# Two unused stretches of memory and eight overwritten products in an attention and mixture kernel

## The chip, the core and the metric

The kernel runs on one core of a Trainium2 chip. The core has a matrix engine (PE, with its weight loads shown apart as PEld), a vector engine (DVE), a scalar engine (ACT), GpSimd (POOL), a queue engine that issues the transfers (SP), an on-chip memory of 128 partitions, and a memory for the sums of the products (PSUM). The metric is the device time of one execution in microseconds; three runs of the kernel before gave 735.54, 736.54 and 736.76 us, a median of 736.54.

## The reference

Attention over 8 batches, 12 heads, 448 positions and 64 columns a head, with scores squeezed by a tanh, and behind it a gated mixture of 768 to 1024 to 512 to 768 columns:

```python
scores = scale * np.matmul(q, k.transpose(0, 1, 3, 2))
scores = cap * np.tanh(scores / cap)
attn = np.exp(scores - max); attn = attn / (sum + 1e-09)
x = (attn @ v) as (batch, 448, 768)
h = np.maximum(x @ w_in, 0.0)
u, v = h[..., :512], h[..., 512:]
v_n = (v - mean(v)) / sqrt(var(v) + 1e-06)
v_s = w_spatial applied over positions to v_n, + b_spatial
out = (u * v_s) @ w_out
```

## The kernel before

A condition on the cap picks one of two forms of the program; the inputs here take the "bounded" one. Each batch has three groups of four heads (`quad_bnd`) and one mixture (`moe`).

In a group the scores are products of 64x64 weights by 448 columns in float32 (L592), ACT takes their tanh (L596) and exponential (L603), and PE multiplies by v (L613). DVE folds the exponentials into maxima and sums (L631, L639, L641); the result goes through memory and comes back as a factor, by which DVE multiplies the group's output (L696). `halves` then splits each pair of heads into a high part (ACT, L353) and a low part (DVE, L349) in a tile `xg`; both parts are numbers of a 32-bit form that PE multiplies in one pass (float32r).

A mixture has four kinds of products, all of full 128x128 weights, three products for each pair of split operands:

- u part (L749 to L751): weights `wi1_h`, `wi1_l`, moving operand `xg`, 448 columns; 4 blocks of 18 products a batch, so 72.
- v part (L771 to L776): weights `xg`, moving operand `wi2_h`, `wi2_l`, 512 columns; 66 a batch.
- spatial part (L840 to L845): weights `vh`, `vl`, moving operand `ws_h`, `ws_l`, 448 columns; 44 a batch.
- output part (L865 to L867): weights `wo_h`, `wo_l`, moving operand `xg`, 448 columns; 72 a batch.

The weights of w_in, w_spatial and w_out are split into their high and low parts in the first batch, by POOL, DVE and ACT, beside the attention (`split_f64`, `split_f32`).

The order of all this is settled when the program is built: `Plan.order` simulates the engines with the costs given to `add`, and takes on each engine the ready task with the lowest key. Each engine then runs its list in that order. A task's function may issue several instructions, which stay together; the task's cost is a number in the call, not counted from them. The first mixture starts with its u part (`V_FIRST` is 1, and the first batch is 0), and its first chain is block j = 0, whose task c = 0 issues three products, then c = 1, and so on; they share the sum tile `acc`.

The tiles of a pool lie one behind the other in each partition, in the order in which they are allocated. Taken modulo 256 bytes, their addresses are these (worked out from the tiles' sizes; every tile that is not named in the change keeps its size):

| tiles | before | with the change |
|---|---|---|
| raw, wi2, ws, red, sh, st | 0 | 0 |
| wi1, wo, dt, one | 0 | 192 |
| v, tp, xf, rr, xg, u, stg | 128 | 0 |
| vh, vl, o | 64 | 192 |

Offsets inside a tile that these products use are multiples of 256 bytes. The distance, modulo 256 bytes and in the shorter direction, between the weights of a product and the operand that streams is therefore: u part 128, then 64; v part 128, then 0; spatial part 64, then 64; output part 128, then 64. In the attention's products (raw with raw, v with tp) it stays as it was.

Of the kernel before, what the change touches and what calls it, by code (L numbers as in the profile page):

```python
# [9 lines left out]
F32 = mybir.dt.float32  # L10
# [6 lines left out]
B, H, S, D = 8, 12, 448, 64  # L17
# [25 lines left out]
class Plan:  # L43
# [15 lines left out]
    def add(self, eng, dur, key, fn, deps=(), uses=(), allocs=(), lat=0.0, name="", mode="N"):  # L59
        t = Task()  # L60
        t.eng, t.dur, t.key, t.fn, t.lat, t.name, t.mode = eng, float(dur), key, fn, lat, name, mode
        t.lock = eng == "P" or eng == "V" and name not in self.OWN
        t.deps = [d for d in deps if d is not None]
        t.allocs = list(allocs)
        t.uses = list(dict.fromkeys(list(uses) + t.allocs))
        for u in t.uses:
            u.users += 1
        t.seq = len(self.tasks)
        self.tasks.append(t)
        return t  # L70
# [123 lines left out]
def act(n, extra=0):  # L194

    return 0.833 * n + 51 + 93 * extra
# [63 lines left out]
               wi5=1.1376, wi6=13.0344, wi7=2.468, wi8=-18.9783, wi9=3.3202, wi10=-13.2504, wi11=-12.154, ws0=-12.654,  # L260
               ws1=-7.9959, ws2=-33.2129, ws3=-10.2049, wo0=-6.4452, wo1=-0.8201, wo2=2.6051, wo3=8.6589)
BND_V_FIRST = 1
WARM, WARM_N = 14, 512
BND_W_KEYS = -14.6272, 0.1578, -3.1507, 14.803, -4.1788, 0.5729, 0.2535
SPARE = ()
PE_SUMS = 3
# [7 lines left out]
def attn_moe(ctx, tc, bounded, shared, qk, v, qk2, v2, cap, w_in, w_sp, w_out, out):  # L274
    nc = tc.nc
# [4 lines left out]
    def pool(name, bufs, space=None):  # L280
        kw = {"space": space} if space else {}
        return ctx.enter_context(tc.tile_pool(name=name, bufs=bufs, **kw))

    const = pool("const", 1)
# [27 lines left out]
    def weights(name, parts, width):  # L312
        return [const.tile([128, parts, width], F32R, name=f"{name}_{p}") for p in "hl"]
# [3 lines left out]
    if bounded:  # L317

        def keep(tag, n, width, fill=None):
            own[tag] = [const.tile([128, width], F32, name=f"{tag}{i}") for i in range(n)]  # L320
            for t in own[tag]:
                if fill is not None:
                    nc.gpsimd.memset(t, fill)

        keep("red", RED, 2 * PW)
        keep("sh", DEN, 64, 1.0)
        keep("st", DEN, 64, 1.0)
    wi1_h, wi1_l = weights("wi1", NP, FH)
    wo_h, wo_l = weights("wo", 4, DM)
    if bounded:  # L330
        keep("dt", DEN, 64, 1.0)
        one = const.tile([128, D + 32], F32, name="one")[:, :D]
        nc.gpsimd.memset(one, 1.0)

    if not bounded:
# [386 lines left out]
    def chain(k, units, acc):  # L722

        prev = None
        for i, (dur, fn, deps, uses) in enumerate(units):
            prev = add("T", dur, k, fn, [prev, *deps], [*uses, acc], [acc] if i == 0 else [], name="moe")
        return prev

    def moe(b, xs):
# [10 lines left out]
        def u_part(js):  # L740
            for j in js:
                k = next(ks)
                acc, u = Buf(next(tags)), Buf("u")
                fs = slice(j * 128, (j + 1) * 128)

                def um(c, acc=acc, fs=fs):
                    x = xs[c][0].t
                    ps = acc.t[:, 0, :S]
                    nc.tensor.matmul(ps, lhsT=wi1_h[:, c, fs], rhs=x[:, XH:], start=(c == 0), stop=False)  # L749
                    nc.tensor.matmul(ps, lhsT=wi1_h[:, c, fs], rhs=x[:, :S], start=False, stop=False)  # L750
                    nc.tensor.matmul(ps, lhsT=wi1_l[:, c, fs], rhs=x[:, XH:], start=False, stop=(c == NP - 1))  # L751

                l = chain(k, [(3 * MM, lambda c=c, um=um: um(c), wi_t[c] + xdep[c], xuse[c:c + 1]) for c in range(NP)], acc)
                r = add("A", act(448), kv(k), lambda acc=acc, u=u: nc.scalar.activation(out=u.t, in_=acc.t[:, 0, :S], func=AF.Relu),
                        [l], [acc], [u], name="urelu")
                us.append((u, r))
# [66 lines left out]
        if b >= V_FIRST:  # L823
            v_part()
            u_part(range(U_LEAD))
        else:
            u_part(range(U_LEAD))
            v_part()
        for j in range(4):
            if j and j + U_LEAD <= 4:  # L830
                u_part([j + U_LEAD - 1])
            k = next(ks)
            acc, gt, g = Buf(next(tags)), Buf("o"), Buf("xg")
            fs = slice(j * 128, (j + 1) * 128)

            def gm(c, acc=acc, fs=fs):
                vh, vl = vs[c][:2]
                ps = acc.t[:, 0, :S]
                if c == 3:
                    nc.tensor.matmul(ps, lhsT=vh.t[:97, fs], rhs=ws_l[:97, c, :], start=False, stop=False)  # L840
                    nc.tensor.matmul(ps, lhsT=vl.t[:, fs], rhs=ws_h[:, c, :], start=False, stop=True)
                    return
                nc.tensor.matmul(ps, lhsT=vh.t[:, fs], rhs=ws_h[:, c, :], start=(c == 0), stop=False)  # L843
                nc.tensor.matmul(ps, lhsT=vh.t[:, fs], rhs=ws_l[:, c, :], start=False, stop=False)  # L844
                nc.tensor.matmul(ps, lhsT=vl.t[:, fs], rhs=ws_h[:, c, :], start=False, stop=False)  # L845

            l = chain(k, [((2 if c == 3 else 3) * MM, lambda c=c, gm=gm: gm(c), ws_t[c] + [vs[c][2]], vs[c][:2])
                          for c in range(4)], acc)
            u, ur = us[j]
            m = add("V", dve(448), kv(k), lambda acc=acc, gt=gt, u=u: nc.vector.tensor_mul(gt.t, acc.t[:, 0, :S], u.t), [l, ur],  # L850
                    [acc, u], [gt], name="gmul")

            e0, e1 = E_G
            c_ = add(e0, ct(e0, 448), kv(k), lambda gt=gt, g=g: copy(e0, g.t[:, XH:], gt.t), [m], [gt], [g], name="gcopy")
            d = add(e1, st2(e1, 448), kv(k), lambda gt=gt, g=g: sub(e1, g.t[:, :S], gt.t, f(g.t[:, XH:])), [c_], [gt, g], name="gl")
            gs.append((g, d))
        for q in range(6):
            k = next(ks)
            acc, o = Buf(next(tags)), Buf("o")
# [30 lines left out]
def either(ctx: ExitStack, tc: tile.TileContext, *args):  # L890
# [24 lines left out]
    with tc.If(bits <= CAP_BITS) as cmp:  # L915
        with ExitStack() as es:
            attn_moe(es, tc, True, shared, *args)
    with cmp.Else():
        with ExitStack() as es:
            attn_moe(es, tc, False, shared, *args)  # L920
# [29 lines left out]
```

## Time and profile before

| | |
|---|---|
| median of 3 runs | 736.54 us (735.54 to 736.76) |
| the profiled execution | 735.65 us |
| its span, first to last instruction | 733.8 us |
| mean granted clock of PE | 0.992 |
| PE busy | 718.4 us (98%) |
| DVE busy | 601.6 us (82%) |
| ACT busy | 480.0 us (65%) |
| POOL busy | 80.9 us (11%) |

The profiled execution is 0.89 us below the median of the runs. A granted clock of 1.00 is 2.4 GHz and 0.50 is 1.2 GHz. Products overlap, so one product's own duration (0.36 us for 448 columns) is longer than the distance from its start to the start of the next (about 0.20 us); what a product costs in a dense stretch is read from that distance.

### The profile page before, as it was taken

How to read it: one execution, taken by the hardware profiler on the slowest of the kernel's cores; microseconds unless marked ns; L12 is line 12 of the kernel's file. 1: busy time of each engine (PE TensorE's matmuls, PEld its weight loads, DVE VectorE, ACT ScalarE, POOL GpSimd, SP SyncE). 2: the span in 40 equal slices, each digit the busy share in tenths (PEclk: the TensorE clock that was granted, in tenths of full speed). 3: DMA queues.
4: the chain of work that ended last, by engine and by line, in shares of the span. 5: the costliest groups of instructions: out<-in, count | busy, mean ns of one | idle time of the engine just before them, and what ended most of it. 6: DMA issues, size and time to landing. Idle time of an engine off the chain costs nothing.

```text
span 733.8 us, 12258 instructions
## 1 busy us (share of the span) xinstructions
PE 718.4 (98%) x4902; PEld 488.2 (67%) x4902; DVE 601.6 (82%) x849; ACT 480.0 (65%) x648; POOL 80.9 (11%) x71
## 2 busy tenths in 40 slices
PE   8996999999999999999999999999999999999997
PEld 3332676575668656786558688568565865698896
DVE  4899999999999989948999996299799688982520
ACT  6999657849784884649875833785876678324321
POOL 2234411600110001000120001000020000200100
PEclk9998999999999999999999999999999999999999
DMA  8565314424221441033330420213321131102002
GB/s 278 163 207 157 111 35 139 161 93 143 69 77 50 132 122 50 26 102 101 101 87 22 155 92 26 63 63 129 101 76 41 60 116 38 52 17 86 1 1 80
DMA packets 34263, 66.50 MB, mean 91 GB/s; under 512 B 6034, under 2 KB 21908, under 8 KB 34196
## 3 DMA queue, kind: packets, MB, share of 16 engines
q1 hardware_dynamic: 34196, 65.62, 28.1%
q8 instruction: 40, 0.66, 0.4%
q14 instruction: 27, 0.22, 0.1%
HBM read 54.40 MB, written 11.18 MB: 89 GB/s over the span
## 4 chain that ended last, share of the span: by engine, by line
PE 88%; DVE 5%; ACT 2%; DMA 2%; issue 1%; SPq 1%; POOL 0%; DVEq 0%; ACTq 0%
PE ps_s L592 15%; PE ps_x L613 15%; PE ps_acc L749 5%; PE ps_acc L750 5%; PE ps_acc L751 5%; PE ps_acc L865 5%; PE ps_acc L866 5%; PE ps_acc L867 5%; PE ps_acc L774 4%; PE ps_acc L776 4%; PE ps_acc L775 4%; PE ps_acc L843 2%; PE ps_acc L844 2%; PE ps_acc L845 2%; DVE red L631 2%; PE ps_acc L771 2%
## 5 line engine op out<-in xcount | busy, mean ns | idle before, releaser
L596 ACT ACTIVATE tp<-ps_s,capt 128x896 f32<-128x896 f32 x168 | 162.5, 1005 | 29.7 <-PE ps_s L592 22.2
L631 DVE TENSOR_TENSOR red<-red,tp 128x1792 f32<-128x1792 f32 x90 | 140.9, 1566 | 23.4 <-ACT tp L603 21.7
L603 ACT ACTIVATE tp<-tp,capt 128x1792 f32<-128x1792 f32 (+1 forms) x96 | 154.1, 1607 | 1.5
L592 PE MATMUL ps_s<-raw 64*64 64x448 f32 x1344 | 146.9, 545 | 3.5 <-ACT tp L596 3.3
L613 PE MATMUL ps_x<-tp,v 64*64 64x448 f32 x1344 | 140.0, 536 | 0.5 <-ACT tp L603 0.4
L631 DVE TENSOR_TENSOR red<-tp 128x1792 f32<-128x1792 f32 x45 | 91.2, 2027 | 13.8 <-ACT tp L603 12.9
L613 PEld LDWEIGHTS ps_x<-tp,v 64*64 64x64 f32 x1344 | 51.2, 133 | 75.9 <-issue 68.7
L592 PEld LDWEIGHTS ps_s<-raw 64*64 64x64 f32 x1344 | 47.4, 133 | 79.3 <-issue 47.5
L798 POOL TENSOR_TENSOR lst<-lst,capt 128x1 f32<-128x1 f32 x32 | 35.0, 1095 | 532.1 <-DVE lst L796 532.0
L749 PE MATMUL ps_acc<-xg,wi_h 128*128 128x448 f32 x180 | 67.5, 375 | 3.1 <-ACT xg L353 3.1
L750 PE MATMUL ps_acc<-xg,wi_h 128*128 128x448 f32 x180 | 66.8, 371 | 0.4 <-DVE xg L349 0.4
L751 PE MATMUL ps_acc<-xg,wi_l 128*128 128x448 f32 x180 | 66.4, 369 | 0.0
L865 PE MATMUL ps_acc<-xg,wo_h 128*128 128x448 f32 x176 | 65.1, 370 | 0.0
L866 PE MATMUL ps_acc<-xg,wo_h 128*128 128x448 f32 x176 | 64.5, 367 | 0.6 <-DVE xg L349 0.6
L867 PE MATMUL ps_acc<-xg,wo_l 128*128 128x448 f32 x176 | 64.4, 366 | 0.0
L353 ACT CAST xg<-o 128x448 fp32r<-128x448 f32 x32 | 18.1, 567 | 53.3 <-DVE o L850 47.8
L774 PE MATMUL ps_acc<-wi_h,xg 128*128 128x512 f32 x126 | 50.6, 402 | 0.0
L639 DVE STREAM_TRANSPOSE red<-red 128x896 f32<-128x896 f32 x45 | 49.6, 1102 | 0.7
L776 PE MATMUL ps_acc<-wi_h,xg 128*128 128x512 f32 x126 | 49.7, 395 | 0.0
L775 PE MATMUL ps_acc<-wi_l,xg 128*128 128x512 f32 x126 | 49.7, 394 | 0.0
L641 DVE TENSOR_REDUCE st<-red 128x28 f32<-128x896 f32 x45 | 48.6, 1079 | 0.7
L631 DVE TENSOR_TENSOR red<-red 128x896 f32<-128x896 f32 x45 | 48.6, 1081 | 0.6
(144 smaller groups left out, 1112.3 us busy)
## 6 DMA issues: line engine op xcount, KB each, us to landing
raw<-in_qk SPq DMA_DIRECT2D x48, 448.0 KB
rr<-rd SPq DMA_DIRECT2D x48, 224.0 KB
out<-o SPq DMA_DIRECT2D x48, 224.0 KB
w<-in_w_in SPq DMA_DIRECT2D x12, 512.0 KB
v<-in_v SPq DMA_DIRECT2D x24, 256.0 KB
v<-in_v SPq DMA_DIRECT2D x24, 192.0 KB
xg<-in_w_out SPq DMA_DIRECT2D x12, 256.0 KB
rd<-dt SPq DMA_DIRECT2D x48, 3.5 KB
```

What stands on the lines that cost most here:

```text
L592: nc.tensor.matmul(ps.t[c * D:(c + 1) * D, e, :S], lhsT=f(raw[c].t)[r, k:k + D], rhs=f(raw[c].t)[r, :S], start=True, stop=True)
L596: th = add("A", act(PW, 1), kk("th", i), lambda ps=ps, tp=tp, o=o: nc.scalar.activation(out=tp.t[:, o:o + PW].rearrange("p (e q) -> p e q" ...
L603: ex = add("A", act_s(w, 1), kk("ex", i), lambda tp=tp, w=w: nc.scalar.activation(out=tp.t[:, :w], in_=tp.t[:, :w], func=AF.Exp, scale=ca) ...
L613: nc.tensor.matmul(x.t[e * D:(e + 1) * D, c, :S], lhsT=vts[g // 2].t[c * D:(c + 1) * D, (4 * (g % 2) + 2 * j + e) * D:(4 * (g % 2) + 2 * j ...
L631: nc.vector.tensor_tensor(o_(), i0(), i1(), op=op)
L749: nc.tensor.matmul(ps, lhsT=wi1_h[:, c, fs], rhs=x[:, XH:], start=(c == 0), stop=False)
L750: nc.tensor.matmul(ps, lhsT=wi1_h[:, c, fs], rhs=x[:, :S], start=False, stop=False)
L751: nc.tensor.matmul(ps, lhsT=wi1_l[:, c, fs], rhs=x[:, XH:], start=False, stop=(c == NP - 1))
L774: nc.tensor.matmul(ps, lhsT=x[:, XH:][:, ts], rhs=wi2_h[:, c], start=(c == 0), stop=False)
L865: nc.tensor.matmul(ps, lhsT=wo_h[:, c, ns], rhs=g[:, XH:], start=(c == 0), stop=False)
L866: nc.tensor.matmul(ps, lhsT=wo_h[:, c, ns], rhs=g[:, :S], start=False, stop=False)
L867: nc.tensor.matmul(ps, lhsT=wo_l[:, c, ns], rhs=g[:, XH:], start=False, stop=(c == 3))
```

## The change

Two things change. A tile `gap` of 192 bytes that nothing reads or writes is allocated between the tiles `st` and `wi1`, and the tile `one`, of which 256 bytes are used, is made 192 bytes longer at its end. So `wi1`, `wo`, `dt` and `one` move by 192 bytes, and all tiles behind `one` by 384 (the table above).

The first task of the first mixture's first chain issues eight more products ahead of its own three: weights `wi1_h` by 448 columns of `wi1_h`, into the chain's sum tile, each started afresh. The chain's own first product starts afresh too and overwrites them. The task's cost in the plan stays as it was, and so does the order of all other instructions.

```diff
-WARM, WARM_N = 14, 512
+WARM, WARM_N, FILL = 14, 512, 8
...
+    if bounded:
+        const.tile([128, 48], F32, name="gap")
     wi1_h, wi1_l = weights("wi1", NP, FH)
     wo_h, wo_l = weights("wo", 4, DM)
...
-        one = const.tile([128, D + 32], F32, name="one")[:, :D]
+        one = const.tile([128, D + 80], F32, name="one")[:, :D]
...
+                fill = FILL if bounded and b == 0 and j == 0 else 0
...
-                def um(c, acc=acc, fs=fs):
+                def um(c, acc=acc, fs=fs, fill=fill):
                     x = xs[c][0].t
                     ps = acc.t[:, 0, :S]
+                    for _ in range(fill if c == 0 else 0):
+                        nc.tensor.matmul(ps, lhsT=wi1_h[:, 0, fs], rhs=wi1_h[:, 0, :S], start=True, stop=True)
                     nc.tensor.matmul(ps, lhsT=wi1_h[:, c, fs], rhs=x[:, XH:], start=(c == 0), stop=False)
```

On PE, at the start of the first mixture, there stood before (raw is the operand of the scores, ps_s their sums):

```order
L592 MATMUL ps_s<-raw_60 64x448 x2
L592 MATMUL ps_s<-raw_61 64x448 x2
L592 MATMUL ps_s<-raw_60 64x448 x2
L592 MATMUL ps_s<-raw_61 64x448 x2
L749 MATMUL ps_acc<-xg,wi_h 128x448
L750 MATMUL ps_acc<-xg,wi_h 128x448
L751 MATMUL ps_acc<-xg,wi_l 128x448
L749 MATMUL ps_acc<-xg,wi_h 128x448
```

Now there stands on PE at the same place (line numbers behind the first edit are 2 to 5 higher):

```order
L594 MATMUL ps_s<-raw_60 64x448 x2
L594 MATMUL ps_s<-raw_61 64x448 x2
L594 MATMUL ps_s<-raw_60 64x448 x2
L594 MATMUL ps_s<-raw_61 64x448 x2
L753 MATMUL ps_acc<-wi_h 128x448 x8
L754 MATMUL ps_acc<-xg,wi_h 128x448
L755 MATMUL ps_acc<-xg,wi_h 128x448
L756 MATMUL ps_acc<-xg,wi_l 128x448
L754 MATMUL ps_acc<-xg,wi_h 128x448
```

The eight products stand between the last scores and the chain's first product. They wait for no other engine: the wait for `xg` stays on the product behind them. On all engines, no other instruction changes its place.

## Rows read from the trace of the kernel before

**Rows 1.** The page: engines' busy time, and the chain that ended last by engine.
```profile
PE 718.4 (98%) x4902; PEld 488.2 (67%) x4902; DVE 601.6 (82%) x849; ACT 480.0 (65%) x648; POOL 80.9 (11%) x71
PE 88%; DVE 5%; ACT 2%; DMA 2%; issue 1%; SPq 1%; POOL 0%; DVEq 0%; ACTq 0%
```

**Rows 2.** Waits of PE, whole span: total us, times, longest us.
```profile
PE ps_s L592 <- ACT tp L596: 3.3, 2, 2.9
PE ps_acc L749 <- ACT xg L353: 3.1, 1, 3.1
...
PE ps_acc L750 <- DVE xg L349: 0.4, 1, 0.4
```

**Rows 3.** Stretches: length, busy us of each engine, granted clock (first after POOL), DMA.
```profile
67.00:69.00 2.00, 1.81 (x12) 0.30 (x8) 2.00 (x6) 2.00 (x2) 0.00 (x0) 0.50 0.03 4
69.00:71.90 2.90, 0.00 (x0) 0.00 (x0) 2.32 (x5) 2.90 (x9) 0.00 (x0) 0.50 0.76 214
74.00:76.90 2.90, 2.90 (x9) 2.60 (x8) 2.90 (x5) 2.87 (x4) 1.50 (x2) 0.50 0.50 200
77.10:152.40 75.30, 74.56 (x536) 47.89 (x534) 74.08 (x128) 50.23 (x72) 22.73 (x17) 1.00 0.33 101
152.40:727.00 574.60, 574.58 (x3760) 412.21 (x3761) 464.68 (x629) 360.39 (x494) 32.37 (x28) 1.00 0.24 74
```

**Rows 4.** PE in order of time, around the first chain: start, duration, idle before.
```profile
66.14 2.67 PE L592 MATMUL ps_s<-raw 64*64 64x448 f32 x16 [2.89 <-ACT tp L596]
71.95 0.74 PE L749 MATMUL ps_acc<-xg,wi_h 128*128 128x448 f32 x1 [3.14 <-ACT xg L353]
73.06 0.74 PE L750 MATMUL ps_acc<-xg,wi_h 128*128 128x448 f32 x1 [0.36 <-DVE xg L349]
73.60 0.57 PE L751 MATMUL ps_acc<-xg,wi_l 128*128 128x448 f32 x1
73.97 0.57 PE L749 MATMUL ps_acc<-xg,wi_h 128*128 128x448 f32 x1
...
76.96 0.41 PE L751 MATMUL ps_acc<-xg,wi_l 128*128 128x448 f32 x1
77.20 0.36 PE L749 MATMUL ps_acc<-xg,wi_h 128*128 128x448 f32 x1
```

**Rows 5.** Waits of DVE from 62 to 153 us, all of them.
```profile
DVE wy L422 <- POOL wy L418: 0.6, 1, 0.6
DVE xg L349 <- ACT xg L353: 0.6, 1, 0.6
DVE vh L809 <- issue: 0.2, 1, 0.2
```

**Rows 6.** Waits of PE from 140 to 153 us; there are none later.
```profile
PE ps_acc L866 <- DVE xg L349: 0.6, 1, 0.6
PE ps_x L613 <- ACT xf L619: 0.2, 1, 0.2
```

**Rows 7.** PE in the last mixture: first and last product of four unbroken stretches.
```profile
674.89 0.39 PE L774 MATMUL ps_s<-wi_h,xg 128*128 128x512 f32 x1
...
690.00 0.40 PE L772 MATMUL ps_acc<-wi_l,xg 128*128 128x512 f32 x1
690.23 0.37 PE L749 MATMUL ps_acc<-xg,wi_h 128*128 128x448 f32 x1
...
697.37 0.37 PE L751 MATMUL ps_s<-xg,wi_l 128*128 128x448 f32 x1
...
709.34 0.37 PE L843 MATMUL ps_s<-ws_h,vh 128*128 128x448 f32 x1
...
713.60 0.37 PE L841 MATMUL ps_s<-ws_h,vl 128*128 128x448 f32 x1
713.80 0.36 PE L865 MATMUL ps_x<-xg,wo_h 128*128 128x448 f32 x1
...
728.28 0.36 PE L867 MATMUL ps_x<-xg,wo_l 128*128 128x448 f32 x1
```

## The prediction

> **What bounds the kernel now.** I read the page's busy times and its chain first: PE is busy 98% of the span and makes up 88% of the chain that ended last [rows 1]. So the question is where PE is not the bound, and at what speed it runs where it is. The list of PE's waits answers the first: two long waits for ACT, of 2.9 and 3.1 us [rows 2], both in the neighbourhood of the first mixture, and then only small ones, the last of them 0.6 us for DVE at about 152 us [rows 6]. The view by stretches puts a border there. From 152.4 to 727 us PE is busy 574.58 of 574.60 us, DVE only 464.68 and ACT 360.39: PE alone is the bound. From 77.1 to 152.4 us both PE (74.56) and DVE (74.08 of 75.30 us) are full [rows 3], and DVE's own waits there name POOL (0.6 us) and issue (0.2 us), never PE or an ACT step that follows PE; its other wait, 0.6 us for ACT, lies before 77 us [rows 5]. So up to 152 us DVE runs at its own pace, splitting weights and folding the attention, and PE stands at the border waiting for a DVE result. What PE saves before the border meets DVE there; what it saves behind it reaches the end.
>
> The clock is the third thing to see. It is 0.50 (1.2 GHz) from 67 us on, after the 2.89 us wait, through the second wait and the first half of the chain, and 1.00 again at 77.1 us [rows 3, 4].
>
> **The eight products.** PE's last scores ahead of the chain run from 66.14 for 2.67 us, so to 68.81. The chain's first product starts at 71.95, after 3.14 us of waiting for ACT [rows 4]. The eight products fall into that hole, since they wait for nobody. At the low clock a product of 448 columns starts every 0.37 us (73.60 to 73.97 in rows 4), so eight take 8 x 0.373 = 2.98 us and end at 71.8 us, 0.15 us ahead of the time at which `xg` is there; if the clock rises on the way they end earlier. Cover: the wait for ACT, which does not depend on PE. If that cover were 0.1 to 0.2 us shorter, the chain would start that much later.
>
> What they give: PE is then busy from 66.14 us nearly without a break. Before, the clock came back at about 77.0 us, after PE had worked without a break since 73.06. With the break filled it should be back by about 71 to 74 us. The second product still waits for DVE until 73.06. From 73.60 to 76.96 there are nine distances of 0.373 us, and one of 0.24 to 77.20 [rows 4]; at the 0.204 us of the full clock (below) the nine save 9 x 0.169 = 1.52 us, and with the distances on either side some 1.8 us. So at 80 us PE should be 1.8 us ahead.
>
> What is late next: DVE. In 77.1 to 152.4 us it has 75.30 - 74.08 = 1.22 us without work. Its listed waits take 0.8 of that, none of them for PE; the rest, 0.4 us, is the most that could shrink if PE's results came sooner. So PE gives the 1.8 us back in waits for DVE (and for ACT behind DVE) before the border. The bounds on what reaches the end are 0.2 us lost (the cover gone, and nothing passed on) and 0.4 us won. I take 0.1 us won, near the low end, since the rows name no wait for PE.
>
> **The two stretches.** They add no instruction. What they can change is the speed of the products whose two operands now lie otherwise to each other. The trace has a natural comparison: before the change the spatial part is 64 bytes apart already, the three others 128. Distances from start to start, in the last mixture, at the full clock [rows 7]: u part, 36 products, (697.37 - 690.23) / 35 = 204.0 ns; output part, 72 products, (728.28 - 713.80) / 71 = 203.9 ns; spatial part, 22 products, (713.60 - 709.34) / 21 = 202.9 ns. All have 448 columns. The v part, 66 products of 512 columns: (690.00 - 674.89) / 65 = 232.5 ns. So a product 64 bytes apart is 1.1 ns faster than one 128 apart, with about 0.5 ns of doubt, since the rows go by 10 ns.
>
> After the change the u and output parts are 64 apart. In the seven mixtures behind the border that is 7 x (72 + 72) = 1008 products, so 1008 x 1.1 = 1.1 us, all on PE where nothing else is the bound. The spatial part stays 64 apart: nothing. The v part goes from 128 to 0 apart, 7 x 66 = 462 products, which no stretch of the trace shows. Its cost is bounded by how much such a product stalls at all: 448 columns at 2.4 GHz are 186.7 ns, so some 17 ns of 204 are lost, and for 512 columns 19 ns of 232.5. At the low clock nothing is lost (0.373 us is 448 columns at 1.2 GHz). If all of it went, the v part would give 462 x 19 = 8.8 us; if it doubled, it would cost as much. As 64 and 128 bytes differ by 1.1 ns only, I take nothing for 0. For the u and output parts the same ends are -1008 x 17 = -17.1 us and +17.1; I take the value of the spatial part, the nearest row. DVE, ACT and the transfers: their tiles move together or by 128 bytes against `red`; for them the bounds are small against the 110 us that DVE has idle behind the border, so I cost them at nothing.
>
> The Trainium skill ("TensorE: Matmul & The Clock Gate", section "Step-by-step: what each phase is for") speaks against any effect: streaming and weight loading have independent read ports, and loading weights takes nothing from a running product. By that rule the second term would be nothing and the sum -0.1 us. The measured 1.1 ns between the parts speaks weakly against the rule, so it stands below as a rival.
>
> **The sum.** -0.1 (eight products) - 1.1 (stretches) = -1.2 us against the profiled execution's 735.65 (733.8 of span and 1.85 around it): 734.45. That execution is 0.89 us under the median, so against the median 736.54 it is 735.3 us.
>
> **Rivals.**
> A is the forecast, 735.3 us, its own range 734.3 to 736.3.
> B: where the operands lie does not matter, and the spatial part is faster for another reason (its sums are shorter, 11 products). Then -0.1: 736.4 us. For it: all four parts lose about the same share, 8 to 9%, whatever their distance. Against it: 1.1 ns is twice the doubt.
> C: DVE is not really the bound up to 152 us, because its instructions shorten when POOL's fall otherwise, and the 1.8 us pass through: 736.54 - 1.8 - 1.1 = 733.6 us. Against it: DVE's 74.08 of 75.30 us, and the wait for it at the border.
> D: the 17 ns stall is mostly a matter of the distance, and 64 in the new direction (weights behind the stream, not ahead of it as in the spatial part) breaks it. If a third goes, 6 ns x 1008 = 6.0 us: 730.4 us; if all of it, about 718. Against it: the spatial part keeps its stall at 64.
> The Trainium skill (same page, section "Back-to-back issue gap") gives columns over 2.4 GHz plus 2.5 ns, which is 189 ns for 448 columns; the trace has 204, so here some of the time stays unexplained by it.
> E, the slower side: the v part at distance 0 has both operands in the same phase and stalls more. If its 19 ns grow by a third, 6.3 ns x 462 = 2.9 us, and with A's gains the sum is +1.7: 738.2 us. It decides from 2.6 ns a product, where the 1.2 us of gains are used up; at 5.8 ns the kernel is slower by more than 0.2%. Without the gain of the u and output parts 3.4 ns are enough for that. For it: no row shows distance 0 in a stretch.
>
> **How the numbers follow.** A 0.42, B 0.22, C 0.10, D 0.09, E 0.17. About 0.2%, 1.47 us, is what a measurement of this kernel can tell from no change, so faster means below 735.07. A straddles that: half of it, 0.21, is faster; with C and D that is 0.40. Same: the other half of A, nearly all of B and 0.01 of E, 0.43. Slower: 0.16 of E and 0.01 of B, 0.17. The range from 732.8 to 738.0 holds A, B, C and about a half of E, and leaves out D and E's upper end, under 2 in 10.
>
> **What would show it.** The stretch 74 to 76.9 us has a granted clock near 1.00 where it was 0.50, and the first chain's products follow at 0.20 us; if not, the eight products do less than I say. PE's waits between 80 and 153 us grow from 0.8 to about 2.5 us, for DVE above all; if they stay as they were, and the whole is 1.8 us shorter, it was C. In the last mixture the u and output parts start every 202.8 ns and the v part every 232.5. Unchanged distances mean B, distances under 198 ns D, a v part over 235 ns E. The prediction is wrong altogether if the stretch behind 152 us shows PE waiting for another engine again.

## The result, and the profile after

The changed kernel takes 728.58 us (median of 4 runs, 728.32 to 729.27) against 736.65 us of the kernel before, run beside it: a ratio of 0.9893, 95% interval 0.9876 to 0.9911, or 8.1 us less. The forecast was 735.3 us with a range from 732.8 to 738.0. The direction was right and the size was far off; of the rivals, D (the distance breaks the stall) comes nearest.

The page of the changed kernel, engines' busy time and the chain that ended last; they answer to [rows 1]. The share of DVE in the chain is 12% where it was 5%, and PE's is 79%, about what the stretch behind the border at 152 us has (574 of 726.5 us): ahead of the border the chain now follows DVE for the most part.

```profile
PE 713.2 (98%) x4910; PEld 487.7 (67%) x4910; DVE 600.4 (83%) x849; ACT 479.9 (66%) x648; POOL 78.4 (11%) x71
PE 79%; DVE 12%; issue 4%; ACT 2%; DMA 1%; SPq 1%; POOL 0%; DVEq 0%; ACTq 0%; POOLq 0%
```

PE around the first chain in the changed kernel (start, duration, idle before), beside [rows 4]. L753 are the eight products. They fill the hole from 68.84 us, and the chain's products follow each other at 0.20 us where they had 0.37.

```profile
66.29 2.62 PE L594 MATMUL ps_s<-raw 64*64 64x448 f32 x16 [2.89 <-ACT tp L598]
68.84 2.74 PE L753 MATMUL ps_acc<-wi_h 128*128 128x448 f32 x8
72.10 0.47 PE L754 MATMUL ps_acc<-xg,wi_h 128*128 128x448 f32 x1 [0.52 <-ACT xg L355]
73.20 0.47 PE L755 MATMUL ps_acc<-xg,wi_h 128*128 128x448 f32 x1 [0.64 <-DVE xg L351]
73.52 0.36 PE L756 MATMUL ps_acc<-xg,wi_l 128*128 128x448 f32 x1
73.72 0.37 PE L754 MATMUL ps_acc<-xg,wi_h 128*128 128x448 f32 x1
```

Stretches of the changed kernel, with the columns of [rows 3]. The clock is back at 1.00 before 71 us. From 77 to 152 us DVE is as full as before (74.19 of 75.30 us).

```profile
69.00:70.60 1.60, 1.60 (x5) 1.43 (x6) 1.27 (x3) 1.60 (x4) 0.00 (x0) 0.50 0.67 169
70.80:71.90 1.10, 0.78 (x4) 0.38 (x2) 1.05 (x2) 1.10 (x5) 0.00 (x0) 1.00 0.78 261
74.00:76.90 2.90, 2.79 (x14) 2.55 (x14) 2.90 (x5) 2.87 (x4) 0.00 (x0) 1.00 0.58 233
77.10:152.40 75.30, 74.27 (x532) 46.98 (x531) 74.19 (x128) 50.66 (x73) 22.60 (x17) 1.00 0.33 102
```

PE's waits from 77 to 153 us in the changed kernel (total us, times, longest); they answer to [rows 5, 6]. They come to 0.8 us, as many as before.

```profile
PE ps_acc L871 <- DVE xg L351: 0.6, 1, 0.6
PE ps_s L594 <- ACT tp L598: 0.2, 1, 0.2
```

DVE's waits in the same stretch. It still waits for nothing that PE makes. Behind 153 us PE waits for no engine.

```profile
DVE wy L424 <- POOL wy L420: 0.6, 1, 0.6
DVE vh L814 <- issue: 0.2, 1, 0.2
```

The same product at the border, on PE, first of the kernel before, then of the changed one. The lead is 152.29 - 151.60 = 0.69 us here.

```profile
152.29 0.47 PE L866 MATMUL ps_acc<-xg,wo_h 128*128 128x448 f32 x1 [0.57 <-DVE xg L349]
```

```profile
151.60 0.48 PE L871 MATMUL ps_acc<-xg,wo_h 128*128 128x448 f32 x1 [0.64 <-DVE xg L351]
```

First and last product of the four unbroken stretches in the last mixture of the changed kernel, beside [rows 7]: v, u, spatial, output.

```profile
668.66 0.39 PE L779 MATMUL ps_s<-wi_h,xg 128*128 128x512 f32 x1
...
683.40 0.39 PE L777 MATMUL ps_acc<-wi_l,xg 128*128 128x512 f32 x1
683.62 0.36 PE L754 MATMUL ps_acc<-xg,wi_h 128*128 128x448 f32 x1
...
690.62 0.36 PE L756 MATMUL ps_s<-xg,wi_l 128*128 128x448 f32 x1
...
702.44 0.36 PE L848 MATMUL ps_s<-ws_h,vh 128*128 128x448 f32 x1
...
706.65 0.36 PE L846 MATMUL ps_s<-ws_h,vl 128*128 128x448 f32 x1
706.85 0.36 PE L870 MATMUL ps_x<-xg,wo_h 128*128 128x448 f32 x1
...
721.05 0.37 PE L872 MATMUL ps_x<-xg,wo_l 128*128 128x448 f32 x1
```

The v part starts every (683.40 - 668.66) / 65 = 226.8 ns where it had 232.5; the u part every 200.0 where it had 204.0; the spatial part 200.5 after 202.9; the output part 200.0 after 203.9. All four are faster, the v part most, and the spatial part too, of which I had expected nothing. The last product of all starts at 721.05 where it was 728.28: 7.23 us of lead, of which 0.69 was there at the border. So 6.5 us come from the faster products behind it, where PE is the bound.

In what follows a part's number is the mean over all its distances behind 79 us, without the few over 0.26 us, which contain a wait. For the kernel before these means are 203.4 (u), 203.9 (output), 202.6 (spatial) and 232.6 ns (v); for the changed kernel 200.0, 200.0, 200.6 and 227.4. With 504, 504, 308 and 462 products in the seven mixtures behind the border, 504 x 3.4 + 504 x 3.9 + 308 x 2.0 + 462 x 5.2 = 6.7 us, about the 6.5 that the trace has.

### The profile page after: what moved, and what is told of

It is laid out like the page before. It is cut to its first block, busy times and chain, and to the rows that moved or that the text cites. A ratio compares the mean times of both kernels' runs of the same rounds, so it can differ in the third digit from the quotient of the medians.

```text
span 726.5 us, 12274 instructions
## 1 busy us (share of the span) xinstructions
PE 713.2 (98%) x4910; PEld 487.7 (67%) x4910; DVE 600.4 (83%) x849; ACT 479.9 (66%) x648; POOL 78.4 (11%) x71
## 4 chain that ended last, share of the span: by engine, by line
PE 79%; DVE 12%; issue 4%; ACT 2%; DMA 1%; SPq 1%; POOL 0%; DVEq 0%; ACTq 0%; POOLq 0%
PE ps_s L594 13%; PE ps_x L615 13%; PE ps_acc L870 5%; PE ps_acc L871 5%; PE ps_acc L872 5%; PE ps_acc L754 4%; PE ps_acc L756 4%; PE ps_acc L755 4%; DVE red L633 4%; PE ps_acc L779 4%; PE ps_acc L780 3%; PE ps_acc L781 3%; PE ps_acc L848 2%; PE ps_acc L850 2%; PE ps_acc L849 2%
## 5 line engine op out<-in xcount | busy, mean ns | idle before, releaser
L754 PE MATMUL ps_acc<-xg,wi_h 128*128 128x448 f32 x180 | 66.2, 368 | 0.5 <-ACT xg L355 0.5
L755 PE MATMUL ps_acc<-xg,wi_h 128*128 128x448 f32 x180 | 65.3, 363 | 0.7 <-DVE xg L351 0.6
```

## The experiments

**Each half alone.** The theory after the result: the address of the weights against that of the streaming operand sets the speed, signed, modulo 256 bytes. The rival: the eight products, by an earlier clock, change something that lasts. First the products alone:

```diff
-    if bounded:
-        const.tile([128, 48], F32, name="gap")
...
-        one = const.tile([128, D + 80], F32, name="one")[:, :D]
+        one = const.tile([128, D + 32], F32, name="one")[:, :D]
```

> The eight products alone, all tiles where they were before. If the distances of the operands made the difference: products of 448 columns start every 203 to 204 ns and of 512 columns every 232 to 233 as before, PE is 1.3 to 1.8 us ahead at 80 us, 0.1 to 0.8 us at 152 us, and that is what the time gains: about 736.0 (735.7 to 736.5). If the eight products made it (an earlier clock that stays better to the end): the products start every 200 and 227 ns and the time is about 728.6.

735.69 us against 735.92, a ratio of 0.9994 (0.9985 to 1.0004). The parts start every 203.4, 203.9, 202.6 and 232.6 ns, as before. The products do their work on the spot, as this row of its stretches shows, and little of it reaches the end. In this trace PE stood 1.11 us behind the kernel before already ahead of the products (a wait for ACT of 3.45 us where it was 2.89), 0.30 ahead at 80 us and 0.52 behind again at 152 us: 1.4 us won by the products, and 0.8 of that given back before the border.

```profile
74.00:76.90 2.90, 2.62 (x12) 2.10 (x12) 2.90 (x5) 2.90 (x4) 0.63 (x1) 1.00 0.82 322
```

Then the stretches alone:

```diff
-WARM, WARM_N, FILL = 14, 512, 8
+WARM, WARM_N, FILL = 14, 512, 0
```

> The two stretches alone, without the eight products. Distances theory: 200.0 ns (u, output), 200.6 (spatial), 227.3 (v) as in the changed kernel, the clock low from 67 to 77 us as before; the time is that of the change and 0 to 0.7 us more: 728.6 to 729.4. Products theory: spacings as before, 736.6.

729.40 us, a ratio of 0.9908 (0.9892 to 0.9923): 6.5 us less than the 735.92 beside it. The parts have the distances of the changed kernel (200.0, 200.0, 200.5, 227.4 ns), with the clock at 0.56 in the stretch from 74 to 76.9 us. The theory of the products falls. The two halves make 0.2 + 6.5 = 6.7 us, and the whole change made 8.1; its interval goes from 6.6 to 9.1 us, so the rest is not clear of the noise.

**Signed distance, or the place of one tile.** Two kernels without the eight products, whose gap and stretch have other sizes: 64 and 192 bytes, then 128 and 0.

```diff
-        const.tile([128, 48], F32, name="gap")
+        const.tile([128, 16], F32, name="gap")
```

> No eight products; gap of 64 bytes, the second stretch 192: wi1 and wo at 64 modulo 256, xg back at 128, vh and vl at 64. Weights minus streaming operand, modulo 256: u and output 192 as in the change, v 128 and spatial 64 as before. Theory of the signed distance: u and output 200.0 ns, v 232.5, spatial 202.6; 1058 x 3.8 ns = 4.0 us less than before, 732.6. Theory of the place of one operand (xg at 0 instead of 128 makes it): all as before, 204 and 232.5 ns, 736.6.

733.11 us, ratio 0.9959 (0.9944 to 0.9974): 2.8 us less, with an interval from 1.9 to 4.1, where I expected 4.0 (the 1058 products of that sum should be 1008, which makes 3.8). Its last mixture, first and last product of the v part and of the output part:

```profile
673.04 0.39 PE L779 MATMUL ps_s<-wi_h,xg 128*128 128x512 f32 x1
...
688.14 0.39 PE L777 MATMUL ps_acc<-wi_l,xg 128*128 128x512 f32 x1
...
711.70 0.36 PE L870 MATMUL ps_x<-xg,wo_h 128*128 128x448 f32 x1
...
725.90 0.37 PE L872 MATMUL ps_x<-xg,wo_l 128*128 128x448 f32 x1
```

Output (725.90 - 711.70) / 71 = 200.0 ns, v (688.14 - 673.04) / 65 = 232.3 ns: the output part is fast although xg lies at 128 as before, and the v part is as slow as before.

```diff
-        const.tile([128, 48], F32, name="gap")
+        const.tile([128, 32], F32, name="gap")
...
-        one = const.tile([128, D + 80], F32, name="one")[:, :D]
+        one = const.tile([128, D + 32], F32, name="one")[:, :D]
```

> No eight products; gap of 128 bytes, second stretch unused: wi1 and wo at 128, xg at 0, vh and vl at 192. Weights minus streaming operand: u and output 128 as before, v 0 and spatial 192 as in the change. Theory of the signed distance: u and output 204 ns, v 227.3, spatial 200.6; 462 x 5.2 + 308 x 2.0 = 3.0 us less than before, 733.6. Theory of the place (xg at 0): u and output 200 ns too, 729 us.

734.07 us, ratio 0.9969 (0.9957 to 0.9981): 1.9 us less, with an interval from 1.4 to 3.2, where I expected 3.0. The same four rows of its trace give the mirror image: output (726.55 - 712.07) / 71 = 203.9 ns, v (688.28 - 673.52) / 65 = 227.1 ns.

```profile
673.52 0.39 PE L779 MATMUL ps_s<-wi_h,xg 128*128 128x512 f32 x1
...
688.28 0.40 PE L777 MATMUL ps_acc<-wi_l,xg 128*128 128x512 f32 x1
...
712.07 0.36 PE L870 MATMUL ps_x<-xg,wo_h 128*128 128x448 f32 x1
...
726.55 0.37 PE L872 MATMUL ps_x<-xg,wo_l 128*128 128x448 f32 x1
```

So it is not where xg lies; each part follows its own signed distance.

**All distances.** Four more pairs of sizes, again without the products (gap and stretch 64 and 128; 0 and 64; 0 and 160; 128 and 224), edited like the last two.

> No eight products; weights minus streaming operand modulo 256: u and output 0, v 64, spatial 0. If the signed distance alone decides, whatever the part (0 fast, 64 and 128 slow, 192 fast, as the earlier runs show for one part each): u and output 200 ns, spatial 200.5, v 230 to 232; 4.0 + 0.6 + 0 to 1.2 us less than before, about 731. If each part has its own best place: u and output anywhere from 200 to 204, v anywhere from 227 to 233.

> No eight products; u and output 64, v 192, spatial 128. Signed distance alone: u and output 202.6 ns, v 226.7 to 227.4, spatial 204; 1.1 + 2.5 - 0.4 = 3.2 us less than before, about 733. Own best places: no such values.

> No eight products; half steps: u and output 224, v 32, spatial 224. If the loss is a smooth function of the signed distance, u, output and spatial stay at 200 ns and v lies between its values at 0 (227.3) and 64 (230 to 232), about 229. If there are steps of 64 bytes: v 227.3 or as at 64.

> No eight products; half steps: u and output 160, v 224, spatial 160. Smooth function: u and output between 204 (at 128) and 200 (at 192), about 202; v 227; spatial 202. Steps of 64 bytes: 200 or 204.

One run each: 737.58, 734.13, 739.40 and 739.92 us, where the kernel before had 737.13, also in one run; what is read from them is the distances. In ns, with those of the other runs (weights minus streaming operand, modulo 256):

| signed distance | u | output | spatial | v (512 columns) |
|---|---|---|---|---|
| 0 | 202.8 | 203.8 | 205.9 | 227.4 |
| 32 | | | | 233.2 |
| 64 | 202.4 | 202.3 | 202.6 | 233.3 |
| 128 | 203.4 | 203.9 | 204.5 | 232.6 |
| 160 | 205.2 | 205.2 | 205.3 | |
| 192 | 200.0 | 200.0 | 200.6 | 229.1 |
| 224 | 205.5 | 206.0 | 205.8 | 233.3 |

My theory in its simple form, one curve for every part, fell with the first of these: at 0 the v part is at its fastest and the three parts of 448 columns are slow, and that kernel won nothing where I expected 4.6 to 5.8 us. What holds is that the three parts of 448 columns agree with each other to about 1 ns, but for distance 0, and have their best place at 192, while 512 columns have it at 0. And the half steps are not between their neighbours, as I had expected, but about as slow as the slower one, or slower.

The means at 0 hide something. There the products of the u and output parts, at the same distance, settle into one of two patterns: 207, 207, 206 ns over and over, or 199, 207, 203, 202, 203 ns with small changes. First and last product of two unbroken stretches of the output part of the first of these kernels:

```profile
596.32 0.36 PE L871 MATMUL ps_acc<-xg,wo_h 128*128 128x448 f32 x1
...
605.82 0.37 PE L872 MATMUL ps_acc<-xg,wo_l 128*128 128x448 f32 x1
662.40 0.36 PE L870 MATMUL ps_acc<-xg,wo_h 128*128 128x448 f32 x1
...
676.79 0.36 PE L872 MATMUL ps_acc<-xg,wo_l 128*128 128x448 f32 x1
```

These are (605.82 - 596.32) / 46 = 206.5 and (676.79 - 662.40) / 71 = 202.7 ns. What picks the pattern no run shows.

**Which weights.** In the u part the high weights come twice and the low weights once. Here only the low ones are moved against the high ones, to a signed distance of 128, while the high ones stand at 192 (for that the tile `one` is 64 bytes shorter than in the kernel before, and `xg` lies at 64).

```diff
-    wi1_h, wi1_l = weights("wi1", NP, FH)
+    wi1_h = const.tile([128, NP, FH], F32R, name="wi1_h")
+    if bounded:
+        const.tile([128, 48], F32, name="gap2")
+    wi1_l = const.tile([128, NP, FH], F32R, name="wi1_l")
+    if bounded:
+        const.tile([128, 16], F32, name="gap3")
```

> No eight products; only the low part of wi1 is moved against the high part, so that in the u part the high weights have a signed distance of 192 to xg and the low weights 128; output part 192, v 64, spatial 0. A u product's own weights and those that are loaded while it streams now differ. If the weights being loaded decide: the slow step is from L750's product to the start of L751's (next weights low), the step from L751 to L749 is fast. If a product's own weights decide: the step after L751 is slow, the one before it fast. Output part 200 ns either way.

735.80 us in one run (v at 64 and spatial at 0 are slow here). Over all u parts, the step from a high product to a low one (own weights at 192, next weights at 128) is 202.9 ns, the step from the low one to the next high one 200.4, and from high to high 201.0. That looks as if the weights that are being loaded counted, but the steps do not carry it. With all weights at 192 (the kernel of 64 and 192 bytes) the same three steps already take 201.1, 200.0 and 199.0 ns, and with all at 64 they take 204.9, 199.6 and 202.3. And the means here mix stretches of several speeds, as at distance 0. First and last product of two u stretches:

```profile
690.78 0.36 PE L757 MATMUL ps_acc<-xg,wi_h 128*128 128x448 f32 x1
...
697.94 0.37 PE L759 MATMUL ps_s<-xg,wi_l 128*128 128x448 f32 x1
706.27 0.36 PE L757 MATMUL ps_acc<-xg,wi_h 128*128 128x448 f32 x1
...
709.67 0.36 PE L759 MATMUL ps_acc<-xg,wi_l 128*128 128x448 f32 x1
```

The first goes at (697.94 - 690.78) / 35 = 204.6 ns, the second at (709.67 - 706.27) / 17 = 200.0, with the same addresses modulo 256. In the slow ones the step into the low product (209 ns) and the step out of it (207 ns) are both slow, in the fast ones neither is. So whether a product's own weights or the next ones count stays open.

**Distance and width by themselves.** In place of the eight products 55 groups of 16, which read wi1_h alone, with the layout of the kernel before:

```diff
+REP = 16
+GRID = [(n, 0, r // 4) for n in (448, 512) for r in range(0, 256, 16)]
+GRID += [(448, (256 - r) % 256 // 4, 0) for r in range(32, 256, 32)]
+GRID += [(n, 8, 8 + r // 4) for n in (448, 512) for r in (0, 64, 128, 192)]
+GRID += [(n, 0, r // 4) for n in (256, 384) for r in (0, 64, 128, 192)]
...
-                    for _ in range(fill if c == 0 else 0):
-                        nc.tensor.matmul(ps, lhsT=wi1_h[:, 0, fs], rhs=wi1_h[:, 0, :S], start=True, stop=True)
+                    if fill and c == 0:
+                        flat = wi1_h.rearrange("p a b -> p (a b)")
+                        for n, s0, w0 in GRID:
+                            for _ in range(REP):
+                                nc.tensor.matmul(acc.t[:, 0, :n], lhsT=flat[:, 1024 + w0:1152 + w0], rhs=flat[:, s0:s0 + n], start=True, stop=True)
```

> The kernel before, with 55 groups of 16 overwritten products in place of the eight, all of weights wi1_h by wi1_h, some 185 us more in all; each group has its own signed distance of weights minus streaming operand (0 to 240 bytes in steps of 16), width (448, 512; four distances each at 256 and 384), and in some groups both operands start 32 bytes off. Read from the distances between starts inside a group. If signed distance and width decide, whatever the tiles: 448 columns 203 to 206 ns at 0, 202.4 at 64, 204 at 128, 200 at 192; 512 columns 227.4 at 0, 233 at 64, 232.6 at 128, 229 at 192. If the parts differ for other reasons (their tiles, the split operands, the summing), the groups at one distance do not repeat these numbers, and 448 and 512 columns have the same best distance. Half steps of 32 bytes are slow (205 to 206) if the distance makes them so; if it is an operand that starts 32 bytes off, the groups with both off are slow at all four distances.

Third and fifteenth product (each row holds two) of five of its groups, in order: 448 columns at 0 and at 192, 512 columns at 0, 64 and 192.

```profile
69.28 0.57 PE L759 MATMUL ps_acc<-wi_h 128*128 128x448 f32 x2
71.76 0.57 PE L759 MATMUL ps_acc<-wi_h 128*128 128x448 f32 x2
...
108.42 0.56 PE L759 MATMUL ps_acc<-wi_h 128*128 128x448 f32 x2
110.82 0.56 PE L759 MATMUL ps_acc<-wi_h 128*128 128x448 f32 x2
...
121.49 0.62 PE L759 MATMUL ps_acc<-wi_h 128*128 128x512 f32 x2
124.21 0.62 PE L759 MATMUL ps_acc<-wi_h 128*128 128x512 f32 x2
...
136.21 0.63 PE L759 MATMUL ps_acc<-wi_h 128*128 128x512 f32 x2
139.01 0.62 PE L759 MATMUL ps_acc<-wi_h 128*128 128x512 f32 x2
...
166.00 0.62 PE L759 MATMUL ps_acc<-wi_h 128*128 128x512 f32 x2
168.75 0.63 PE L759 MATMUL ps_acc<-wi_h 128*128 128x512 f32 x2
```

Over twelve distances these are 206.7, 200.0, 226.7, 233.3 and 229.2 ns. Over the last 13 distances of a group:

| signed distance | 0 | 16 | 32 | 64 | 96 | 128 | 160 | 192 | 224 | 240 |
|---|---|---|---|---|---|---|---|---|---|---|
| 448 columns | 206.7 | 206.7 | 204.5 | 202.0 | 200.1 | 204.2 | 205.3 | 199.8 | 206.3 | 203.3 |
| 512 columns | 226.7 | 226.6 | 233.5 | 233.2 | 234.3 | 233.7 | 232.8 | 228.9 | 233.3 | 226.8 |

The six distances left out of the table have 202.9 to 204.8 and 229.9 to 233.6 ns. The curve of the parts returns, to about 1 ns, with no xg, no low parts and no summing: signed distance and width decide. The exception is 448 columns at 0, where the groups have the slower of the two patterns and the u and output parts mostly the other. Nor is every half step slow, as I had expected: 96 is fast. Moving the stream instead of the weights puts the two 256 bytes nearer to each other and gives the same numbers (200.0 at 96, 199.8 at 192, 206.6 at 224), which is what "modulo 256" rests on. With both 32 bytes off, 448 columns have 206.6, 202.0, 203.8 and 200.2 ns at 0, 64, 128 and 192, and 512 columns 229.2, 233.5, 232.4 and 228.7 (the first one settles late; its last five distances have 226.6): the place of an operand by itself does nothing that shows. The changed kernel has 448 columns at 192 and 512 columns at 0, the best or nearly the best of the curve for each; by this curve no other pair of sizes would beat it by more than 0.1 ns a product.

**Where the products' gain goes.** Two kernels with the old layout, without and with the eight products, in which DVE does less: two instructions of each of the 12 blocks of the w_out split are left out, so the weights' values are not those of w_out.

```diff
-            ("V", dve2(n), lambda: V.tensor_scalar(yu(), yu(), 3, None, op0=ALU.logical_shift_left)),
-            ("V", dve(n), lambda: V.scalar_tensor_tensor(yu(), w3()[:, :, 1], 0x80000000, yu(), op0=ALU.bitwise_and,
+            ("V", dve2(n), lambda: None if late else V.tensor_scalar(yu(), yu(), 3, None, op0=ALU.logical_shift_left)),
+            ("V", dve(n), lambda: None if late else V.scalar_tensor_tensor(yu(), w3()[:, :, 1], 0x80000000, yu(), op0=ALU.bitwise_and,
```

> The kernel before with 24 DVE instructions of the w_out split left out (two of each of its 12 blocks, 8.2 us by the rows of before, nearly all between 76 and 153 us; the weights' values are then not those of w_out). PE's order is unchanged. If DVE is what PE waits for up to the border, PE's wait of 0.6 us at 152 us goes, and little else: 735.3 to 736.2 us. If DVE is not the bound there: as before.

735.12 us against 735.73, ratio 0.9988 (0.9976 to 1.0000). PE has no wait at all from 77 to 153 us, and its lead on the kernel before jumps from -0.05 to 0.8 us at the border and stays: DVE was what PE waited for.

> The same with the eight products (the same instructions of the w_out split left out). If DVE's pace before the border took back what the eight products won, the 1.5 us now pass: 1.2 to 1.6 us less than the kernel with less DVE work alone, where with all of DVE's work the products won 0.2 us. If they were lost in another way: again about 0.2 us.

733.80 us, ratio 0.9967 (0.9954 to 0.9981): 1.3 us less than the kernel without the products, as expected, where with all of DVE's work they won 0.2. The two intervals overlap, so this supports the reason and does not settle it. The traces support it too: with all of DVE's work PE's lead fell by 0.7 us (whole change) and 0.9 us (products alone) from 80 to 140 us, and with less of it the lead holds, 0.39 us at 80 and 0.40 at 140. But in this profiled execution the products themselves won nothing (PE's lead was 0.55 us before them and 0.39 at 80 us), for this reason:

```profile
69.50:72.80 3.30, 1.73 (x8) 1.02 (x6) 2.72 (x5) 3.30 (x10) 0.91 (x1) 1.00 0.83 274
72.90:76.20 3.30, 3.23 (x9) 2.92 (x10) 3.30 (x6) 3.27 (x5) 0.00 (x0) 0.50 0.68 245
```

There the clock came back at 69.5 us, PE then had only 1.73 of 3.30 us of work while it waited for `xg`, and the clock fell to 0.50 once more until 76.2 us.

## Why the prediction was wrong

**The bound.** Right. PE alone is the bound behind 152 us, and DVE's pace before it; leaving out DVE work removed the wait at the border. The sign that I named for PE giving its lead back there did not come: PE's listed waits did not grow from 0.8 to about 2.5 us. The lead fell all the same, from 1.33 us at 80 to 0.64 at 140 us, in its largest step (0.37 us, at 138 us) at scores that wait for ACT, of which the list shows 0.2 us; a product that starts late while the one before it still runs does not count as a wait there.

**The eight products.** The mechanism was right, the size roughly. They fill the hole, the clock is back before 71 us, and PE gains about 1.5 us by 80 us (I said 1.8). I let 0.1 us pass, with 0.4 as the upper end; alone they won 0.2 us, with an interval from 1.1 us faster to 0.3 slower. The lead of 0.69 us at the border does not size them, since the stretches alone have 0.54 there. Counted from the scores ahead of the products, one trace each, PE gains up to the border 0.83 us with the whole change, 0.59 with the products alone and 0.26 with the stretches alone:

```profile
152.82 0.47 PE L869 MATMUL ps_acc<-xg,wo_h 128*128 128x448 f32 x1 [0.59 <-DVE xg L349]
151.76 0.48 PE L871 MATMUL ps_acc<-xg,wo_h 128*128 128x448 f32 x1 [0.64 <-DVE xg L351]
```

(The border's product with the products alone, then with the stretches alone.) So the upper end of 0.4 was perhaps too tight. In the whole change DVE's instructions from 60 to 153 us took 0.32 us less in all (a `dt` step went from 0.43 to 0.18 us), which would be a part of rival C; that was read from the traces and not tried.

**The stretches.** Here it failed, in two sentences of the step. I wrote that the u and output parts would take "the value of the spatial part, the nearest row", and that the spatial part "stays 64 apart: nothing". Both take the distance in the shorter direction, without its sign. Before the change the spatial part's weights lie 64 bytes ahead of the stream; after it the weights of all three parts lie 64 behind it, at 192. The runs show 202.6 ns at 64 and 200.0 to 200.6 at 192. So the term of 1.1 ns was 3.4 to 3.9, and the spatial part's nothing was 2.0. I had the sign in hand, and put it into rival D, with 0.09.

The second failure is the v part. I reasoned from 64 and 128 differing by 1.1 ns that 0 would do nothing; it does 5.2 ns, over 462 products the largest single share a product has. No row showed that distance in a stretch. Two points on a curve were taken for its whole shape. Of rival E, which named the same distance, the sign was wrong.

**The rivals.** B falls: the distance matters for every part. Where the weights lie against the stream changes a product's time by up to 6.9 ns of 200 (199.8 to 206.7 at 448 columns). The Trainium skill's rule on the independent ports ("TensorE: Matmul & The Clock Gate", section "Step-by-step: what each phase is for"), by which the stretches would do nothing, is not what the runs show for these products. D was right in kind: a fifth to a quarter of the 17 ns went, not a third. Its sign, distances under 198 ns, did not come either; 200.0 lies between it and the 202.8 of A. Its other end, about 718 us, is 719.3 by its own terms (736.54 - 0.1 - 17.1). The best distances are 11.0 ns over the columns for 256 columns and 13.1 to 13.3 for 384 to 512. The Trainium skill's gap of columns over 2.4 GHz plus 2.5 ns (same page, section "Back-to-back issue gap"), which it gives for a product by itself, is reached at no distance here.

**The range.** It had bounds of 17 us on either side for the unknown cost, and used hardly any of them. With a cost that no row showed, the range should have reached D.

## What to carry to other kernels

Where PE runs full-size float32r products back to back, the address of the weights against that of the streaming operand, signed and modulo 256 bytes, is worth a sweep: here it moved a product's time by 1 to 2% (over the whole curve by up to 3.5%), and the kernel's by 0.9%. A mean can hide two patterns at one distance, so the single distances are worth a look. The best distance depends on the product's width, so sweep with the widths that the kernel has, and with products that nobody reads, before choosing the sizes of unused tiles. A gain on one engine is worth what the engine that is late next lets through, and that engine must be looked up stretch by stretch.

## What was not expected of the hardware

For 384, 448 and 512 columns the best distances are nearly the same amount over the columns: 173.3, 200.0 and 226.7 ns are each 13.3 ns more than the columns at 2.4 GHz. That is 32 cycles, an estimate worked out from these numbers; what they are spent on no run shows. 256 columns have 120.0 ns at 0, the same amount, but go under it at 64 (117.7) and at 192 (117.8).

At a bad distance the time is not evenly longer: the starts of 448 columns at 128 repeat 209, 196, 203, 212, 200 ns, at 192 they repeat 201, 201, 198. At the low clock, at a distance of 128, products of 448 columns started every 373 ns [rows 4], which is the columns alone at 1.2 GHz, so at that distance nothing of this shows there. Why 448 columns are best at 192 and at 96 and 512 columns at 0 stays open.
